# An attention and feed-forward block on one core: down weights scaled by the gate row once and kept in memory, three more copy buffers, fewer warming matmuls in the first stage

## The chip, the core and the metric

The kernel runs on one core of one Trainium2 chip. A core has a matrix engine (TensorE, PE in the profile), a vector engine (VectorE, DVE), an engine for functions such as exp (ScalarE, ACT), GpSimd (POOL) and SyncE (SP), which issues nearly all transfers here. The metric is the device time of one execution in microseconds; less is better. The time given for a kernel is the median of several executions.

## The reference, cut to what matters

One transformer block with 2048 tokens of width 512, 32 heads of 16 columns, a feed-forward width of 1792, and six modulation rows that come from a condition `c`. All inputs are bfloat16.

```python
mod = (_silu(c) @ w_mod).reshape(1, 6, 1, -1)
sa, ca, ga, sb, cb, gb = (mod[:, k] for k in range(6))
h = _layernorm(x) * (1 + ca) + sa
q, k, v = heads(h @ wqkv)                       # 32 heads of 16 columns
p = softmax(q @ k.T / 4)
x = x + ga * ((p @ v) @ wo)
h = _layernorm(x) * (1 + cb) + sb
x = x + gb * ((gelu(h @ w_gate) * (h @ w_up)) @ w_down)
```

The change touches the last line. `gb` is a row of 512 numbers that multiplies the columns of the product with `w_down`, so it can be multiplied into the columns of `w_down` just as well.

## The kernel before

**Stages.** The prologue (`prologue`, from line 524) loads x, the modulation weights and the first columns of `wqkv`, normalises four token tiles, computes `sa` and `ca` as columns (`mod_cols`), transposes, and projects the first queries and keys. Matmuls on a zero tile (`warm_up`: 5, 11, 4 and 3 of them, 512 columns each) stand between its parts. Then `stream` runs through 2048 score tiles (128 keys by 512 columns) in a fixed order: first the pairs of heads of the first 512 queries, then query sets of 256 tokens, at last two sets of 128 (`SETS`, nine sets, numbered 0 to 8). A "round" is four such tiles, one for each of four heads that share the array. `tail` finishes the last set.

**Two ways to the exponential.** Most score tiles are taken out of PSUM by ScalarE, two or three tiles to an ACTIVATE (`E<-ps_sc`, line 341). Some rounds are given to VectorE instead. Such a round, called a vector round below (`quad` in the code), is four TENSOR_SCALARs of 128x512, which turn each score into the bits of a bfloat16 power of two (into a buffer of `self.kq`), and three TENSOR_SCALARs of 128x2048, which make three shifted copies of those bits (`shift_task`, each into a buffer of `self.sq`, the copy buffers). The product with v is then done four times, on the bits and on the three copies with three scaled versions of v (`vs`), which averages out the error of the cheap exponential. A copy buffer comes free when its product has been issued.

**The copy buffers.** There are six: three in `mreg`, one of its own, one in `ereg` and one in the upper half of `onorm`. `room` in `stream` says which may be used: numbers 3, 4, 5 for the first two units, 3 and 4 until the second modulation is computed, and then 0 to 3, with number 4 for the first four units as well.

**The order of the work** is decided when the program is built. A planner in `stream` keeps a modelled clock for each engine (`model`, `cost`) and takes at each step the work that could run then: the next score tiles, a product with v, or one step of the side work (`plan`: projections, the output projection `side_wo`, the feed-forward `side_ffn`), which has a credit that grows with the tiles done. Steps for VectorE and for the transfers wait in a list of tasks (`task`), sorted by `urgency`. A new vector round is begun only if VectorE is free soon, its list is short, a `kq` buffer is free, and no other condition in that long `elif` forbids it. The instructions then run in that order on each engine, with semaphores.

**The feed-forward.** Sets 0 to 5 (`FLOW` is 6) run while the attention of later sets still needs the memory, so for each of them the gate, up and down weights are loaded again from HBM in pieces (`load`, `load_down`; a down piece is 256 rows, 256 KB, into `wdst`). Sets 6 to 8 use weights that stay in memory, loaded late by `weight_parts`. The gate row is applied in two ways. For sets 0 to 5 `down_fin` multiplies the 128x512 result in PSUM by `gb` into `xw` and adds `xw` to x. For sets 6 to 8 `scale_down` multiplies the fourteen resident 128x512 tiles of down weights by `gb` on VectorE when they have arrived (tasks `("wds", i)`), and `down_fin` adds the PSUM result to x directly.

```python
    def down_fin(self, bank, t, flow=False):
        if flow:
            self.tt("dve", self.xw, bank, self.gb[:, :], ALU.mult)
        self.tt("dve", self.xs[:, t, :], self.xs[:, t, :], self.xw if flow else bank, ALU.add)
```

The seventh pieces of the resident gate and down weights go to `hreg`, behind the products of the feed-forward, and may be loaded after set 0's feed-forward (in the run: around 612 and 620 us); pieces 4 to 6 of the up weights and piece 5 of the down weights wait for set 5's feed-forward (around 701 us).

Of the kernel before, what the change touches and what calls it, by code (L numbers as in the profile page):

```python
# [6 lines left out]
ALU = mybir.AluOpType  # L7
BF16 = mybir.dt.bfloat16
# [40 lines left out]
AHEAD = (30, 44)  # L49
FLOW = sum(a + n <= 1536 for a, n in SETS)  # L50
URGENT = 9
LATE = 2
# [8 lines left out]
TUNE = ((600, 3500, 6, 120),) * 16  # L61
# [31 lines left out]
class _Recorder:  # L93
# [167 lines left out]
    def model(self, op, t, cost):  # L261
# [6 lines left out]
        elif eng == "pe":  # L268
# [11 lines left out]
            end = t + max(cols + (12 if mode else 6), 64) / 2.4  # L280
# [153 lines left out]
class _Kernel(_Recorder):  # L434
# [12 lines left out]
    def alloc(self):  # L447
# [40 lines left out]
        self.sq += [ereg[:, :], onorm[:, 2048:4096]]  # L488
# [6 lines left out]
        self.xw = self.gw[:, 0, 0, 0:D]  # L495
# [19 lines left out]
        self.ones = dreg[:, 10 * D:10 * D + P]  # L515
        self.half = dreg[:, 10 * D + P:10 * D + 2 * P]
# [4 lines left out]
        self.scr2 = self.dram("scr_rec", [4, 2048], FP32)  # L521


    def prologue(self):
# [52 lines left out]
        self.warm_up(4)  # L577
        self.mod_cols(self.scp[:, 1, 0:8], 0, range(4))
        self.warm_up(3)
# [347 lines left out]
    def weight_parts(self):  # L927
# [5 lines left out]
        dv = self.B_w_down.rearrange("(f p) n -> p f n", p=P)  # L933
# [7 lines left out]
        return ([piece(0, i, g[i]) for i in range(6)] + [piece(0, 6, g[6], [("ffn", 0)]), piece(2, 6, d[6], [("ffn", 0)])]  # L941
# [20 lines left out]
    def scale_down(self):  # L962

        for i in range(NFC // 2):
            self.task([lambda fc=fc: self.tt("dve", self.wd[fc // 2][:, fc % 2, :], self.wd[fc // 2][:, fc % 2, :], self.gb[:, :], ALU.mult)
                       for fc in (2 * i, 2 * i + 1)], ("wds", i), self.after([("wr", 2, i)]))

# [144 lines left out]
    def side_ffn(self, gi, part=None):  # L1112
# [116 lines left out]
        for i in range(n):  # L1229
            for fc in range(NFC):  # L1230
                yield from self.until(("wl", gi, 2, fc // 2) if flow else ("wds", fc // 2))
                yield 512, lambda i=i, fc=fc: self.mm(
                    mi, prod[:, fc, P * i:P * i + P], (self.wdst if flow else self.wd)[fc // 2][:, fc % 2, :], start=(fc == 0), stop=(fc == NFC - 1))
            self.down_fin(mi, tiles[i], flow)
# [8 lines left out]
    def urgency(self, tk):  # L1243
# [3 lines left out]
        if tk[1] is not None and tk[1][0] == "shift" and self.plain[tk[1][1]] <= LATE:  # L1247
            return -2
# [774 lines left out]
```

## Time and profile before

| | |
|---|---|
| median of 3 runs | 818.45 us (818.15 to 819.36) |
| span of the profiled execution, first to last instruction | 817.5 us |
| ACT busy | 783.2 us (96%) |
| PE busy | 750.5 us (92%) |
| DVE busy | 742.8 us (91%) |
| mean granted TensorE clock | 1.000 |
| DMA, mean over the span | 70 GB/s |

The profile gives the profiled execution by its span alone, which is 0.95 us below the median of the runs. In the rows, a line is "start, length, engine, source line, operation, output<-input, shape, count", and a bracket tells how long the engine was idle before it and what ended that. Tiles are called by the memory they lie in: `E<-ps_sc` is ScalarE's exponential; `dreg`, `kq`, `mreg` or `onorm` `<-ps_sc` with 128x512 uint16 is the first part of a vector round; 128x2048 uint16 is one of its three copies; `wreg<-ps_mi,gb` is the multiplication in `down_fin`, and `xs<-xs,gb` and `hreg<-hreg,gb` are those of `scale_down`. Nearly every operation goes through a helper, so the source line names the helper (328 is a matmul, 341 an ACTIVATE, 353 a TENSOR_SCALAR, 345 a TENSOR_TENSOR), and groups are told apart by their tiles.

### The profile page before, as it was taken

What the parts mean: (1) busy time and instruction counts of PE and PEld (TensorE: products, weight loads), DVE (VectorE), ACT (ScalarE), POOL (GpSimd) and SP (SyncE); (2) the same over time, 40 slices, a digit from 0 to 9 for tenths busy, and PEclk for the clock granted to TensorE, in tenths of its full rate; (3) what the DMA queues carried; (4) which work ended last, traced back from release to release, by engine and by line L of the source; (5) the groups of instructions that cost most, each with busy time, mean ns of one, the idle gap of its engine ahead of it and who ended that gap; (6) DMA issues with size and microseconds to landing.
All of it is one profiled execution on the core that took longest, in us unless ns stands there. A gap on an engine that the chain in (4) does not pass through costs nothing.

```text
span 817.5 us, 37365 instructions
## 1 busy us (share of the span) xinstructions
PE 750.5 (92%) x17184; PEld 366.4 (45%) x17188; DVE 742.8 (91%) x1496; ACT 783.2 (96%) x746; POOL 4.6 (1%) x13
## 2 busy tenths in 40 slices
PE   7899999998999898989999899998998899888998
PEld 3333334343543454435443444444443444346567
DVE  6876898899999999999999999999999999989874
ACT  5999999999999999999999999999999999999962
POOL 2000000000000000000000000000000000000000
PEclk9999999999999999999999999999999999999999
DMA  9100000021530153104420442034233541200000
GB/s 292 63 6 20 10 9 10 10 71 40 168 112 16 52 155 93 35 21 134 122 63 16 136 121 61 16 105 133 63 106 88 165 126 36 67 10 10 19 13 14
DMA packets 94499, 57.38 MB, mean 70 GB/s; under 512 B 17029, under 2 KB 91910, under 8 KB 94342
## 3 DMA queue, kind: packets, MB, share of 16 engines
q1 hardware_dynamic: 93812, 54.47, 23.6%
q8 instruction: 134, 2.20, 1.2%
q10 hardware_dynamic: 530, 0.53, 0.2%
q14 instruction: 23, 0.19, 0.1%
HBM read 50.04 MB, written 2.35 MB: 64 GB/s over the span
## 4 chain that ended last, share of the span: by engine, by line
ACT 88%; PE 9%; DVE 1%; issue 0%; DMA 0%; SPq 0%; DVEq 0%
ACT E L341 85%; PE ps_sc L328 4%; PE ps_mi L328 3%; ACT wreg L341 3%; PE ps_pv L328 2%; DMA xs<-in_A_x_dram 0%; DVE osb L362 0%; DVE xs L345 0%; DVE dreg L353 0%; DVE st L381 0%; DVE wreg L353 0%; DVE nwt L345 0%; PE ps_sc L332 0%; DVE wreg L358 0%; DVE mreg L353 0%
## 5 line engine op out<-in xcount | busy, mean ns | idle before, releaser
L341 ACT ACTIVATE E<-ps_sc 128x1024 bf16<-128x1024 f32 (+2 forms) x700 | 758.7, 1319 | 19.1 <-PE ps_sc L328 19.0
L328 PE MATMUL ps_sc<-qT,kT 32*128 32x256 bf16 (+3 forms) x2048 | 202.2, 273 | 25.2 <-ACT E L341 21.1
L328 PE MATMUL ps_sc<-qo,kT 32*128 32x256 bf16 (+2 forms) x2048 | 202.2, 273 | 16.9 <-ACT E L341 15.5
L328 PE MATMUL ps_pv<-E,vaug 128*17 128x256 bf16 (+2 forms) x3204 | 154.1, 273 | 3.8 <-DVE osb L362 2.7
L353 DVE TENSOR_SCALAR dreg<-ps_sc 128x512 uint16<-128x512 f32 x200 | 135.5, 687 | 6.8 <-PE ps_sc L328 5.8
L328 PE MATMUL ps_mi<-wreg,mreg 128*32 128x256 bf16 x2816 | 116.6, 275 | 6.5 <-DVE wreg L362 3.4
L328 PEld LDWEIGHTS ps_sc<-qT,kT 32*128 32x128 bf16 (+1 forms) x2048 | 62.3, 92 | 117.3 <-ACT E L341 105.1
L328 PEld LDWEIGHTS ps_sc<-qo,kT 32*128 32x128 bf16 x2048 | 62.1, 92 | 105.6 <-ACT E L341 94.9
L328 PEld LDWEIGHTS ps_pv<-E,vaug 128*17 128x17 bf16 x3204 | 60.4, 89 | 59.6 <-issue 39.8
L328 PEld LDWEIGHTS ps_mi<-wreg,mreg 128*32 128x32 bf16 x2816 | 63.7, 96 | 42.8 <-issue 24.8
L328 PE MATMUL ps_pv<-mreg,vs 128*17 128x256 bf16 (+2 forms) x1840 | 80.9, 268 | 0.6 <-DVE mreg L353 0.3
L353 DVE TENSOR_SCALAR kq<-ps_sc 128x512 uint16<-128x512 f32 x104 | 70.9, 688 | 8.6 <-PE ps_sc L328 8.2
L353 DVE TENSOR_SCALAR mreg<-dreg 128x2048 uint16<-128x2048 uint16 x100 | 67.5, 682 | 2.2 <-PE ps_pv L328 2.2
L353 DVE TENSOR_SCALAR mreg<-ps_sc 128x512 uint16<-128x512 f32 x96 | 65.0, 688 | 4.5 <-PE ps_sc L328 4.3
L328 PEld LDWEIGHTS ps_pv<-mreg,vs 128*17 128x17 bf16 x1840 | 40.7, 91 | 15.1 <-issue 4.7
L353 DVE TENSOR_SCALAR mreg<-mreg 128x2048 uint16<-128x2048 uint16 x71 | 47.4, 686 | 0.0
L328 PE MATMUL ps_mi<-hreg,wreg 128*32 128x512 bf16 (+1 forms) x496 | 36.6, 376 | 0.4 <-DVE vaug L362 0.3
L362 DVE CAST wreg<-ps_mi 128x512 bf16<-128x512 f32 x49 | 33.6, 686 | 2.4 <-PE ps_mi L328 2.2
L345 DVE TENSOR_TENSOR wreg<-wreg 128x1024 bf16<-128x1024 bf16 (+1 forms) x56 | 34.5, 618 | 0.0
L353 DVE TENSOR_SCALAR sq<-dreg 128x2048 uint16<-128x2048 uint16 x49 | 33.7, 687 | 0.8 <-PE ps_pv L328 0.8
L358 DVE SCALAR_TENSOR_TENSOR wreg<-wreg,ps_mi 128x512 bf16<-128x512 bf16 x49 | 33.4, 682 | 1.0 <-ACT wreg L341 0.5
L353 DVE TENSOR_SCALAR mreg<-kq 128x2048 uint16<-128x2048 uint16 x48 | 32.5, 683 | 0.0
(193 smaller groups left out, 722.7 us busy)
## 6 DMA issues: line engine op xcount, KB each, us to landing
mreg<-in_B_w_up_dram SPq DMA_DIRECT2D x46, 256.0 KB, 3.2
mreg<-in_B_w_gate_dram SPq DMA_DIRECT2D x42, 256.0 KB, 3.3
dreg<-in_B_w_down_dram SPq DMA_DIRECT2D x18, 256.0 KB, 3.5
rb<-scr_rec SPq DMA_DIRECT2D x120, 32.0 KB, 2.0
mreg<-in_B_w_down_dram SPq DMA_DIRECT2D x12, 256.0 KB, 3.7
ereg<-in_B_w_down_dram SPq DMA_DIRECT2D x12, 256.0 KB, 3.8
mreg<-in_w_mod_dram SPq DMA_DIRECT2D x1, 2048.0 KB, 11.8
out_dram<-xs SPq DMA_DIRECT2D x15, 128.0 KB, 1.7
```

The lines of the kernel that those rows point to most:

```text
L328: return self.rec("pe", lambda e: e.matmul(out, lhsT, rhs, start=start, stop=stop, tile_position=tp), [lhsT, rhs], [out], cost=(n, int(rhs ...
L341: return self.rec("act", lambda e: e.activation(out, in_, func, scale=scale, **kw), rd, wr, cost=self.cost("act", out, [in_], "act"))
L345: return self.rec(eng, lambda e: e.tensor_tensor(out, a, b, op), [a, b], [out], cost=self.cost(eng, out, [a, b], "tt"))
L353: return self.rec(eng, lambda e: e.tensor_scalar(out, a, s1, s2, **kw), rd, [out], cost=self.cost(eng, out, [a], "ts") + 60 * (len(rd) - 1 ...
L358: return self.rec("dve", lambda e: e.scalar_tensor_tensor(out, a, s, b, op0=op0, op1=op1), rd, [out], cost=self.cost("dve", out, [a, b], " ...
L362: return self.rec(eng, lambda e: e.tensor_copy(out, in_), [in_], [out], cost=self.cost(eng, out, [in_], "ts"))
```

## The change

- **Down weights.** Set 0's feed-forward loads the down weights as before, multiplies each of the seven pieces in place by `gb` (two TENSOR_TENSORs of 128x512 a piece), and stores the piece to a new tensor `wd_scaled` in HBM. Sets 1 to 5 and the resident copy load from there. `scale_down` is gone, and `down_fin` adds PSUM to x directly for every set.
- **Copy buffers.** Three more: number 6 in `hreg` behind the products, 7 in the part of `mreg` that is down buffers 3 and 4, and 8 in the part of `dreg` that is down buffers 1 and 2. Rules say when each may be used: 8 is added to the early lists and, with 4, to the list until the last query projection is done; 6 is added from there to the end of set 5's feed-forward; 4 and 7 after that. Set 0's loads of down pieces 1, 2, 5 and 6 wait until numbers 8 and 4 are free. The seventh resident gate and down pieces now wait for the end of set 5's feed-forward and for number 6. The constants `ones` and `half` move out of `dreg` to tiles of their own.
- **First stage.** Of the last three warming calls (11, 4 and 3 matmuls) 11 and 1 are left.
- **The planner.** The model takes a full-array matmul as at least 158 columns long (it was 64 for all kinds). The planner's constants are gathered in a tuple that may differ for every 64 score tiles; all its entries have the values of before.

```diff
-        self.sq += [ereg[:, :], onorm[:, 2048:4096]]
+        self.sq += [ereg[:, :], onorm[:, 2048:4096], hreg[:, NFC * 256:NFC * 256 + 2048], mreg[:, 10240:12288], dreg[:, 10 * D:14 * D]]
...
-            end = t + max(cols + (12 if mode else 6), 64) / 2.4
+            end = t + max(cols + (12 if mode else 6), 64 if mode else 158) / 2.4
...
         self.warm_up(11)
         self.mod_cols(self.scp[:, 1, 0:8], 0, range(4, 8))
-        self.warm_up(4)
+        self.warm_up(1)
         self.mod_cols(self.scp[:, 1, 0:8], 0, range(4))
-        self.warm_up(3)
         self.ln_rstd(0, 4)
...
-        return ([piece(0, i, g[i]) for i in range(6)] + [piece(0, 6, g[6], [("ffn", 0)]), piece(2, 6, d[6], [("ffn", 0)])]
+        return ([piece(0, i, g[i]) for i in range(6)] + [piece(0, 6, g[6], [last, "sq"]), piece(2, 6, d[6], [last, "sq"])]
...
-    def down_fin(self, bank, t, flow=False):
-        if flow:
-            self.tt("dve", self.xw, bank, self.gb[:, :], ALU.mult)
-        self.tt("dve", self.xs[:, t, :], self.xs[:, t, :], self.xw if flow else bank, ALU.add)
+    def down_fin(self, bank, t):
+        self.tt("dve", self.xs[:, t, :], self.xs[:, t, :], bank, ALU.add)
...
-                v = self.B_w_down.rearrange("(f p) n -> p f n", p=P)
-                self.task([("sp", lambda: self.dma("sp", self.wdst[i], v[:, 2 * i:2 * i + 2, :], "sd%d" % i))], ("wl", gi, 2, i))
+                v = self.wdg if gi else self.B_w_down.rearrange("(f p) n -> p f n", p=P)
+                steps = [("sp", lambda: self.dma("sp", self.wdst[i], v[:, 2 * i:2 * i + 2, :], "sd%d" % i))]
+                if not gi:
+                    steps += [lambda x=x: self.tt("dve", self.wdst[i][:, x, :], self.wdst[i][:, x, :], self.gb[:, :], ALU.mult) for x in range(2)]
+                    steps += [("sp", lambda: self.dma("sp", self.wdg[:, 2 * i:2 * i + 2, :], self.wdst[i], "ws%d" % i))]
+                self.task(steps, ("wl", gi, 2, i),
+                          (lambda: NSQ in self.sq_free) if i > 4 else (lambda: NSQ + 4 in self.sq_free) if i in (1, 2) else None)
...
             if u in units[:2]:
-                ok = (3, 4) if pool is self.quad_free else (3, 4, 5)
+                ok = (3, 4) if pool is self.quad_free else (3, 4, 5, 8)
             elif "modB" not in self.have:
-                ok = (3,) if pool is self.quad_free else (3, 4)
+                ok = (3,) if pool is self.quad_free else (3, 4, 8)
+            elif pool is self.quad_free:
+                ok = range(NK)
             else:
-                ok = range(NK if pool is self.quad_free else NSQ + (u in units[:4]))
+                ok = list(range(NSQ))
+                if ("ffn", FLOW - 1) in self.have:
+                    ok += [NSQ, NSQ + 3]
+                elif ("q", 3, NDC - 1) in self.have:
+                    ok += [NSQ + 2]
+                elif ("t2T", 0) not in self.have:
+                    ok += [NSQ, NSQ + 4]
```

More of the change, by code (lines that the diff above doesn't have):

```diff
@@ L514, in alloc @@
         self.zero = sb("zero", [P, P], BF16)
-        self.ones = dreg[:, 10 * D:10 * D + P]
-        self.half = dreg[:, 10 * D + P:10 * D + 2 * P]
+        self.ones = sb("ones", [P, P], BF16)[:, :]
+        self.half = sb("half", [P, 2], BF16)[:, :]
         self.self32 = sb("self32", [P, P], FP32)
@@ L960, in scale_wo @@
         yield
[L962 to L966, printed above, removed]
     def normed(self, k, i):
@@ L1246, in urgency @@
             return -3
-        if tk[1] is not None and tk[1][0] == "shift" and self.plain[tk[1][1]] <= LATE:
+        if tk[1] is not None and tk[1][0] == "shift" and self.plain[tk[1][1]] <= self.tune[6]:
             return -2
@@ L1293, in background @@
             pass
-        while self.free["dve"] <= t + 150 and self.step("dve", max(self.free["dve"], t) + 40):
+        while self.free["dve"] <= t + self.tune[13] and self.step("dve", max(self.free["dve"], t) + 40):
             pass
@@ L1547, in stream @@
         parts = self.weight_parts()
-        self.scale_down()
         while cg <= group[units[-1]]:
+            if ("ffn", FLOW - 1) in self.have and NSQ + 2 in self.sq_free:
+                self.done("sq")
             if parts and pos >= max(loaded, ends[FLOW - 1] + 8):
@@ L1557, in stream @@
             t = max(self.pe_now(), virt)
-            self.tune = TUNE[min(pos // P, 15)]
+            if pos // STEP != stage:
+                stage = pos // STEP
+                self.rules(stage)
             for k in range(NSETS):
```

40 lines of the change are left out of this document (21 added, 19 removed).

## The prediction

> **What bounds the kernel now.** I read the page's head and its chain first, then the chain in order of time, then a table by stage, since the shares of the whole run (ACT 96%, PE 92%, DVE 91%) leave open which engine sets the time where.
>
> ```profile
> span 817.5 us, 37365 instructions
> ACT 88%; PE 9%; DVE 1%; issue 0%; DMA 0%; SPq 0%; DVEq 0%
> ...
> 16.45 101.58 ACT E L341 x93
> ...
> 669.72 60.76 ACT E L341 x56
> ...
> 736.01 5.45 ACT E L341 x5
> 741.50 0.62 PE ps_sc L328 x12
> ```
>
> ```profile
> core 0: us, PE busy (x) PEld busy (x) DVE busy (x) ACT busy (x) POOL busy (x), PEclk, DMA share, GB/s
> 40.00:100.00 60.00, 55.50 (x1036) 20.90 (x1036) 44.98 (x102) 60.00 (x57) 0.31 (x1) 1.00 0.05 12
> 100.00:200.00 100.00, 93.96 (x2115) 39.94 (x2114) 91.85 (x174) 99.02 (x92) 0.00 (x0) 1.00 0.10 23
> 200.00:700.00 500.00, 464.17 (x10794) 223.77 (x10791) 484.19 (x913) 500.00 (x476) 0.00 (x0) 1.00 0.32 89
> 700.00:740.00 40.00, 34.59 (x832) 17.83 (x832) 35.19 (x73) 40.00 (x36) 0.00 (x0) 1.00 0.14 40
> 740.00:790.00 50.00, 45.45 (x1620) 29.37 (x1612) 42.11 (x91) 46.37 (x43) 0.00 (x0) 1.00 0.07 13
> ```
>
> There are three stages. Up to 16.45 us a chain of all engines leads to the first exponentials. From there to 741 us ScalarE is busy without a pause, but for 1 us near 118, so the time of this stage is the sum of ScalarE's work. From 741.5 the chain runs through TensorE, and ScalarE has gaps (46.37 busy of 50). In the long middle stage only less work for ScalarE shortens the run, and such work can only go to VectorE, by vector rounds. Whether more of them are made depends on VectorE: it is full from 200 to 700 (484.19 of 500) but idle for 15.0 us between 40 and 100 and for 8.2 us between 100 and 200.
>
> **The price of a vector round.**
>
> ```profile
> L341 ACT ACTIVATE E<-ps_sc 128x1024 bf16<-128x1024 f32 x432 | 434.9, 1169 | 2.0 <-PE ps_sc L328 2.0
> L341 ACT ACTIVATE E<-ps_sc 128x1536 bf16<-128x1536 f32 x260 | 385.9, 1591 | 3.8 <-PE ps_sc L328 3.8
> ```
>
> ```profile
> L328 PE MATMUL ps_pv<-mreg,vs 128*17 128x256 bf16 (+2 forms) x1840 | 80.9, 268 | 0.6 <-DVE mreg L353 0.3
> L353 DVE TENSOR_SCALAR kq<-ps_sc 128x512 uint16<-128x512 f32 x104 | 70.9, 688 | 8.6 <-PE ps_sc L328 8.2
> L353 DVE TENSOR_SCALAR mreg<-dreg 128x2048 uint16<-128x2048 uint16 x100 | 67.5, 682 | 2.2 <-PE ps_pv L328 2.2
> ```
>
> In a step with a vector tile the ACTIVATE has two tiles in place of three: 1591 - 1169 = 422 ns less. A round is four tiles, so it takes 4 x 0.422 = 1.69 us from ScalarE. It costs VectorE 4 x 0.688 + 3 x 0.682 = 4.80 us. It costs TensorE three more products with v; at width 256 these are 24 matmuls of 80.9/1840 = 0.044 us, 1.06 us.
>
> **The change part by part.**
>
> *Warming matmuls (six of seven gone).*
>
> ```profile
> 8.67 1.02 PE L328 MATMUL ps_mi<-dreg 128*128 128x512 bf16 x4
> 9.53 0.54 PE L328 MATMUL ps_sc<-sc_bf,mreg 128*128 128x1 bf16 x16
> 10.15 0.59 PE L328 MATMUL ps_mi<-dreg 128*128 128x512 bf16 x2
> 10.58 0.72 PE L332 MATMUL ps_sc<-ident,dreg 128*128 128x128 bf16 x10
> ```
>
> ```profile
> DMA to landing us min/median/max: 6.8/6.9/7.0
> ```
>
> ```profile
> 1.81 0.47 SPq L391 DMA_DIRECT2D mreg<-in_w_mod_dram  x1
> ...
> 8.52 1.05 DVE L353 TENSOR_SCALAR dreg<-xs,mv,rstd 128x512 bf16<-128x512 bf16 x3
> ...
> 8.63 0.81 ACT L341 ACTIVATE dreg<-xs,nwt,rstd 128x512 bf16<-128x512 bf16 x1 [2.98 <-DVE nwt L358]
> ...
> 11.85 0.28 PE L328 MATMUL ps_sc<-hreg,wreg 128*128 128x256 bf16 x1 [0.21 <-ACT hreg L341]
> ...
> 14.33 1.45 ACT L341 ACTIVATE E<-ps_sc 128x1536 bf16<-128x1536 f32 x1 [0.58 <-PE ps_sc L328]
> ```
>
> These matmuls lie on the chain. The second half of the modulation columns (9.53) waits for four of them, the transposes (10.58) for the other three. Without them that half waits for its weights: issued at 1.81 us and landing 7.0 us later (the row on landing gives the two such transfers), at 8.8 us, so it starts near 8.9 and ends near 9.45. The transposes then wait for the normalised tiles, ready at 9.57 on VectorE and 9.44 on ScalarE. They start near 9.55 and not 10.58: 1.0 us less to the first exponential, now at 14.33. The ends are 0 (something later, such as the query weights, binds) and 1.03; I take 1.0, since the row nearest to a limit, the tiles at 9.57, has been counted.
>
> The trace shows the clock rise during the 11 matmuls that stay: their lengths fall from 634 to 380 ns.
>
> ```profile
> L328 PE MATMUL ps_mi<-dreg x6: 608/634/634, 3.7 to 5.8; 128*128 128x512 bf16 x6
> ...
> L328 PE MATMUL ps_mi<-dreg x3: 379/380/427, 7.1 to 7.6; 128*128 128x512 bf16 x3
> ```
>
> The Trainium skill (TensorE: Matmul & The Clock Gate, Part 1) says that the clock halves again only after an idle window of about 3.4 us; by that the gain stays 1.0. Its Part 4 speaks against the change: transposes do not count as busy in the same way, and transposes take the place of the warming matmuls. Rival 3 is what that would cost here.
>
> *Multiplication by the gate row.*
>
> ```profile
> L345 DVE TENSOR_TENSOR wreg<-ps_mi,gb x12: 680/683/692, 252.9 to 699.4; 128x512 bf16<-128x512 f32 x12
> L345 DVE TENSOR_TENSOR xs<-xs,gb x12: 366/420/422, 625.3 to 713.3; 128x512 bf16<-128x512 bf16 x12
> ```
>
> The rows give the shortest, median and longest length in ns, and the first and last start. Twelve multiplications out of PSUM go: 12 x 0.683 = 8.2 us of VectorE, two per set of sets 0 to 5. The fourteen on the weights (twelve in this row, two more on the piece in `hreg`) are not removed but moved, from 625 to 713 us to set 0's feed-forward, ahead of its first result at 252.9: 14 x 0.420 = 5.9 us there, and as much less later. In both places VectorE is full, so 1.2 rounds (5.9/4.80) are lost and won, which I cost at nothing. The 8.2 us are worth 8.2/4.80 = 1.7 rounds, 2.9 us at most and 0 at least (if the planner leaves them idle). Rounds are whole and the time comes in pieces of 1.4 us per set, so I take one, 1.7 us.
>
> *Traffic for the scaled weights.*
>
> ```profile
> dreg<-in_B_w_down_dram SPq DMA_DIRECT2D x18, 256.0 KB, 3.5
> ```
>
> Seven stores of 256 KB are added on SP's queue, in a stage where the DMA share is 0.32; behind them stand the loads of the next pieces and the small transfers of the softmax sums. A load of such a piece takes 3.5 us to land, and set 1 reads the stored pieces most of a set later; a set takes about (699.4 - 252.9)/5 = 89 us. Cost nothing; without that cover one landing, 3.5 us. Set 0's down matmuls now wait for load and scaling; what hides this is the gate and up work ahead of them. The added waits for buffers 4 and 8 come after these have ceased to be given out, so they cost nothing, or again one landing.
>
> *Late pieces of the resident weights.*
>
> ```profile
> 700.95 1.98 SPq L391 DMA_DIRECT2D dreg<-in_B_w_up_dram  x1
> ...
> 720.78 0.69 DVE L362 CAST wreg<-ps_mi 128x512 bf16<-128x512 f32 x1 [1.35 <-PE ps_mi L328]
> ```
>
> Two more pieces now go ahead of the up pieces issued at 700.95, spaced by eight score tiles each, about 6 us by 2048 tiles in some 775 us. The up pieces would land near 711; set 6's feed-forward takes its first gate result at 720.78 and uses those pieces later. Nothing.
>
> *Copy buffers.* Three or four in place of two or three before 95 us, six in place of four or five up to about 185 us, five in place of four until 700, then six. Where VectorE is full they add nothing. Between 40 and 200 us it is idle for 23.2 us, room for 4 whole rounds (23.2/4.80), 6.8 us; at least 0, and less than nothing is excluded by TensorE's idle time there (4.5 + 6.0 us against 1.06 a round). How much of the idle time is due to buffers can't be read directly:
>
> ```profile
> 87.46 0.69 DVE L353 TENSOR_SCALAR ereg<-kq 128x2048 uint16<-128x2048 uint16 x1
> ...
> 88.95 0.69 DVE L353 TENSOR_SCALAR sq<-kq 128x2048 uint16<-128x2048 uint16 x1
> ```
>
> Here the third copy of a round came 0.8 us late, into the buffer that the first had left, so the buffers do bind, if shortly; most of the gaps wait for TensorE. By that nearest row I take one round, 1.7 us.
>
> *The planner's 158 columns* move no work, only its order; I take 0, with an end of one ACTIVATE, 1.6 us, to either side.
>
> **The sum.** 1.0 + 1.7 + 1.7 = 4.4 us less: a span of 813.1, and with the 0.95 us by which the span lies below the median of the runs, 814.0.
>
> **The rivals.**
>
> 1. *The end grows.* From 741 us TensorE sets the time, and a vector round there gives nothing to it and costs. With six buffers in place of four, more rounds find room: VectorE has 4.8 us idle from 700 to 740 and 7.9 from 740 to 790, enough for two whole rounds.
>
> ```profile
> L328 PE MATMUL ps_pv<-mreg,vs 128*17 128x128 bf16 (+1 forms) x216 | 5.4, 221 | 0.0
> ...
> DVE mreg L353 <- PE ps_pv L328: 2.1, 1, 2.1
> ```
>
> At width 128 a round costs TensorE 48 x 5.4/216 = 1.2 us, and at most all its 4.80 us on VectorE, if they stand ahead of the feed-forward's steps for which TensorE waits. Two rounds are 2.4 to 9.6 us; the forecast is eaten up and the run is slower by 0.2% from 3.0 us a round. Taking 4.0, the time is 822. For it: copies waited for a buffer here (2.1 us). Against: at 1.2 us it does not decide.
>
> 2. *Nothing is made of it.* VectorE's freed time and the buffers bring no round, because the begin of a round is forbidden by other conditions. Then only the first stage gains: 817.5. For it: most idle time of VectorE before 100 us ends with TensorE, not with a buffer.
>
> 3. *The clock falls back* after the transposes. From the transposes at 10.58 to the first exponential at 14.33 are 3.75 us; were all of them TensorE's, they would take 634/380 as long, 2.5 us more: 816.5. Against it: the matmul of 256 columns at 11.85, right after the transposes, takes 0.28 us, which is not a slow length beside 0.38 for 512.
>
> 4. *Much more of it.* All four rounds before 200 us and two from the freed time: 818.45 - 1.0 - 6 x 1.69 = 807.3.
>
> **How the numbers follow.** The forecast has 0.48, rival 1 0.24, rival 2 0.14, rival 3 0.04, rival 4 0.10. Within 0.2% (1.6 us) is about what a measurement of this kernel can't tell from no change; so faster is 0.48 + 0.04 + 0.10 = 0.62, same 0.14, slower 0.24. The forecast's own range is 811 to 816.5 (one round more or none, 1.6 us of order). For 8 in 10 it reaches to rival 1 at 822 and towards rival 4, to 808.5, which leaves out about half of each beyond.
>
> **What would show it.** The first exponential should start near 13.3 and not 14.33. The rows with `ps_mi,gb` should be gone, and fourteen of 0.42 us stand before 253 us. The TENSOR_SCALARs of 128x512 uint16 out of `ps_sc` should be 8 more than before (two rounds), and the ACTIVATEs of 1536 columns fewer. ScalarE's unbroken stretch should end 4 us earlier, near 737, and the last 76 us keep their length. The prediction is wrong if the count of rounds falls, or if that last stretch grows by 4 us or more.

## The result, and the profile after

The changed kernel is slower by 0.3%: 822.23 us, the median of 20 runs (819.64 to 827.39), against 819.42 us for the kernel before beside it (20 runs, 818.15 to 823.71); the ratio is 1.0032, with a 95% interval of 1.0017 to 1.0047. Forecast were 814.0 us, and the time lies just above the end of the range, 822.0. The profiled execution is one of the best of the changed kernel: 819.71 us, a span of 818.0 us at a mean granted clock of 0.998, against a span of 817.5 at 1.000 before.

The page's head, its busy times and the shares of its chain:

```profile
span 818.0 us, 37375 instructions
...
PE 749.4 (92%) x17194; PEld 366.7 (45%) x17194; DVE 737.7 (90%) x1484; ACT 783.6 (96%) x746; POOL 4.6 (1%) x13
...
ACT 76%; PE 17%; DVE 5%; DMA 1%; issue 1%; SPq 0%; DVEq 0%
```

The chain names ScalarE for 76% of the span; before it was 88%. Yet ScalarE has the same work as before (783.6 us against 783.2), and VectorE has 5.1 us less (737.7 against 742.8). The groups by shape show what became of the freed time: every kind of exponential has its old count.

```profile
L340 ACT ACTIVATE E<-ps_sc 128x1024 bf16<-128x1024 f32 x432 | 434.7, 1169 | 7.3 <-PE ps_sc L327 7.2
L340 ACT ACTIVATE E<-ps_sc 128x1536 bf16<-128x1536 f32 x260 | 384.4, 1597 | 2.3 <-PE ps_sc L327 2.3
...
L352 DVE TENSOR_SCALAR dreg<-ps_sc 128x512 uint16<-128x512 f32 x200 | 134.7, 684 | 10.4 <-PE ps_sc L327 9.6
L352 DVE TENSOR_SCALAR kq<-ps_sc 128x512 uint16<-128x512 f32 x104 | 70.2, 684 | 8.7 <-PE ps_sc L327 8.2
L352 DVE TENSOR_SCALAR mreg<-ps_sc 128x512 uint16<-128x512 f32 x96 | 64.6, 683 | 3.0 <-PE ps_sc L327 2.4
...
L352 DVE TENSOR_SCALAR onorm<-ps_sc 128x512 uint16<-128x512 f32 x4 | 2.7, 672 | 1.6 <-PE ps_sc L327 1.6
```

200 + 104 + 96 + 4 are 404 tiles, 101 rounds, as many as before. No round has been made of VectorE's freed time or of the new buffers. What changed on ScalarE is the wait: 7.3 us ahead of the ACTIVATEs of 1024 columns, where it was 2.0 (ahead of those of 1536 columns 2.3, where it was 3.8). The table by stage (same columns as before) shows where:

```profile
40.00:100.00 60.00, 54.59 (x1016) 20.33 (x1008) 44.77 (x103) 60.00 (x57) 0.31 (x1) 1.00 0.05 12
100.00:200.00 100.00, 94.24 (x2151) 40.80 (x2152) 92.89 (x177) 98.12 (x91) 0.00 (x0) 1.00 0.10 23
200.00:700.00 500.00, 461.25 (x10764) 223.49 (x10760) 478.09 (x897) 497.59 (x473) 0.00 (x0) 1.00 0.33 91
700.00:740.00 40.00, 36.34 (x868) 18.11 (x867) 36.00 (x75) 40.00 (x37) 0.00 (x0) 1.00 0.20 53
740.00:790.00 50.00, 45.77 (x1574) 29.18 (x1568) 42.18 (x92) 46.66 (x43) 0.00 (x0) 1.00 0.07 16
```

Between 40 and 740 us ScalarE, unbroken before but for 1 us, is now idle for 1.88 + 2.41 = 4.29 us. The start and the end of the exponentials, from the timeline (start, length):

```profile
7.84 0.54 PE L327 MATMUL ps_sc<-sc_bf,mreg 128*128 128x1 bf16 x16
...
8.65 1.03 PE L331 MATMUL ps_sc<-ident,dreg 128*128 128x128 bf16 x10 [0.27 <-DVE dreg L352]
...
12.71 1.45 ACT L340 ACTIVATE E<-ps_sc 128x1536 bf16<-128x1536 f32 x1 [0.58 <-PE ps_sc L327]
...
792.08 1.28 ACT L340 ACT_TABLE_LOAD   x1
```

The kernel before has the same table load, behind its last exponential, at 789.52:

```profile
789.52 1.28 ACT L341 ACT_TABLE_LOAD   x1
```

So the profiled executions compare like this. The first exponential is 1.62 us earlier (12.71 against 14.33). ScalarE loses 4.29 - 0.98 = 3.3 us more to waits between 40 and 740, and 0.7 us in a stretch of halved clock near 21 us (below). Its own work is 0.4 us longer and its idle time from 740 to 790 is 0.3 shorter. That makes 2.5 us, and the end of the exponentials is 2.56 us later. From there to the end the changed kernel needs 25.9 us and not 28.0, which leaves the 0.5 us between the spans.

Most of the middle stage's loss lies in one stretch. Counted by the starts of the instructions that take score tiles out of PSUM, the changed kernel is 0.2 us ahead at tile 512 and 3.3 us behind at tile 704. Of the 192 tiles between, VectorE takes 38 and not 43, which is 5 x 0.42 = 2.1 us more for ScalarE, and ScalarE waits for 1.25 us, where it did not wait before. From tile 1536 to 1920 VectorE takes 84 tiles and not 78, so that the count of the whole run is the same.

### The profile page after: what moved, and what is told of

Its sections match the earlier page's. It is cut to its first block, busy times and chain, and to the rows that moved or that the text cites. A ratio compares the mean times of both kernels' runs of the same rounds, so it can differ in the third digit from the quotient of the medians.

```text
span 818.0 us, 37375 instructions
## 1 busy us (share of the span) xinstructions
PE 749.4 (92%) x17194; PEld 366.7 (45%) x17194; DVE 737.7 (90%) x1484; ACT 783.6 (96%) x746; POOL 4.6 (1%) x13
## 4 chain that ended last, share of the span: by engine, by line
ACT 76%; PE 17%; DVE 5%; DMA 1%; issue 1%; SPq 0%; DVEq 0%
ACT E L340 73%; PE ps_sc L327 7%; PE ps_mi L327 6%; PE ps_pv L327 4%; ACT wreg L340 3%; DVE dreg L352 1%; DVE mreg L352 1%; DVE kq L352 1%; DMA scr_rec<-rden 1%; DMA xs<-in_A_x_dram 0%; DVE wreg L361 0%; DMA rb<-scr_rec 0%; DVE wreg L357 0%; DVE st L380 0%; DVE osb L361 0%
## 5 line engine op out<-in xcount | busy, mean ns | idle before, releaser
L327 PE MATMUL ps_sc<-qT,kT 32*128 32x256 bf16 (+3 forms) x2048 | 193.7, 273 | 26.3 <-ACT E L340 22.2
L327 PE MATMUL ps_sc<-qo,kT 32*128 32x256 bf16 (+2 forms) x2048 | 193.4, 273 | 15.0 <-ACT E L340 13.6
L327 PEld LDWEIGHTS ps_sc<-qT,kT 32*128 32x128 bf16 (+1 forms) x2048 | 59.6, 92 | 117.8 <-ACT E L340 103.3
L327 PEld LDWEIGHTS ps_sc<-qo,kT 32*128 32x128 bf16 x2048 | 59.5, 92 | 103.9 <-ACT E L340 90.6
L327 PE MATMUL ps_pv<-mreg,vs 128*17 128x256 bf16 (+2 forms) x1472 | 62.8, 268 | 1.0 <-DVE mreg L352 0.9
L352 DVE TENSOR_SCALAR mreg<-dreg 128x2048 uint16<-128x2048 uint16 x90 | 60.3, 680 | 0.0
L327 PEld LDWEIGHTS ps_pv<-mreg,vs 128*17 128x17 bf16 x1472 | 32.9, 91 | 11.1 <-issue 4.0
L352 DVE TENSOR_SCALAR mreg<-mreg 128x2048 uint16<-128x2048 uint16 x47 | 31.7, 682 | 0.0
L361 DVE COPY osb<-ps_pv 128x256 f32<-128x256 f32 (+2 forms) x63 | 25.9, 412 | 5.5 <-PE ps_pv L327 5.4
L340 ACT ACTIVATE wreg<-wreg 128x1024 bf16<-128x1024 bf16 (+1 forms) x28 | 30.8, 1099 | 0.0
```

What stands on the lines that cost most here:

```text
L327: return self.rec("pe", lambda e: e.matmul(out, lhsT, rhs, start=start, stop=stop, tile_position=tp), [lhsT, rhs], [out], cost=(n, int(rhs ...
L340: return self.rec("act", lambda e: e.activation(out, in_, func, scale=scale, **kw), rd, wr, cost=self.cost("act", out, [in_], "act"))
L352: return self.rec(eng, lambda e: e.tensor_scalar(out, a, s1, s2, **kw), rd, [out], cost=self.cost(eng, out, [a], "ts") + 60 * (len(rd) - 1 ...
L361: return self.rec(eng, lambda e: e.tensor_copy(out, in_), [in_], [out], cost=self.cost(eng, out, [in_], "ts"))
```

## The experiments

Each kernel ran several times beside the kernel before on the same chip; a ratio is to that, with its 95% interval, and below 1 is faster. "Planned again" says that the planner ran again and was free to make a new order of the whole kernel; "order kept" says that instructions were taken out or put in after the planning and all others stayed in place.

### Each part of the change by itself

The modelled columns, undone in the changed kernel (e1), and alone in the kernel before (e2):

```diff
-            end = t + max(cols + (12 if mode else 6), 64 if mode else 158) / 2.4
+            end = t + max(cols + (12 if mode else 6), 64 if mode else 64) / 2.4
```

> The changed kernel with one thing undone: the planner's model takes a full-array matmul as at least 64 columns again, as before. The work is the same, only its order is planned anew. Theory R (the new order, brought about by the 158 columns, costs the time): about 3 us less than the changed kernel, near 819 us. Theory C (the missing warming matmuls let TensorE's clock fall) and theory S (the scaling in set 0's stage costs the time): as the changed kernel, near 822 us, with a mean granted clock near 0.994.

> The kernel before with one thing of the change alone: 158 columns in the planner's model. Theory R: 3 to 5 us slower than before, near 823 us, with fewer vector rounds than 101. Theories C and S: within 1 us of before, 819.4.

e1 took 821.40 us, 1.0015 (0.9995 to 1.0034), with 102 rounds, which can be told neither from the kernel before nor from the changed one. e2 took 825.86 us, 1.0068 (1.0046 to 1.0089), with 99 rounds. This constant belongs to the planner's model and to no instruction, so it only orders the work; but the order also decides how many rounds VectorE gets, and e2's two fewer rounds leave ScalarE more to do (788.0 us against 783.2). Alone the constant costs more than the whole change does.

Fewer warming matmuls alone (e3), planned again, and the changed kernel with them back (e4):

```diff
-        self.warm_up(4)
+        self.warm_up(1)
...
-        self.warm_up(3)
```

> The kernel before with one thing of the change alone: six of the last seven warming matmuls left out. Theory C: the first exponential starts 1.6 us earlier (12.7 in place of 14.3 us), but the mean granted clock falls below 0.997 in most executions and the time is 1 to 3 us above before, near 821. Theories R and S: the 1.6 us are kept, 817.8 us, with the clock as in the kernel before.

> The changed kernel with one thing undone: the calls of 4 and 3 warming matmuls are back. Theory C: the first exponential is 1.6 us later, at 14.3 us, but the clock stays above 0.997 in most executions; the median is near 821, below that of the changed kernel (822.2), and the executions lie closer together. Theories R and S: the 1.6 us are added and nothing is won back, 823.8 us.

e3 took 820.93 us, 1.0022 (1.0000 to 1.0044), at a mean granted clock of 0.9931, which is what theory C expected, but in a new order. e4 took 823.10 us, 1.0032 (1.0014 to 1.0051). In e4 the planner happened to arrive at the order of the changed kernel: VectorE, ScalarE and the transfers have the same instructions in the same order, and so has TensorE but for ten more matmuls in the first stage, six of warming and four that fill. So e4 tests the matmuls of the first stage alone, and its clock, 0.9945, is as low as the changed kernel's 0.9942. The missing warming matmuls do not cause the lower clock.

The scaled down weights alone (e5) and the three copy buffers alone (e6), both on the kernel before and planned again:

```diff
-                v = self.B_w_down.rearrange("(f p) n -> p f n", p=P)
+                v = self.wdg if gi else self.B_w_down.rearrange("(f p) n -> p f n", p=P)
...
+                if not gi:
+                    steps += [lambda x=x: self.tt("dve", self.wdst[i][:, x, :], self.wdst[i][:, x, :], self.gb[:, :], ALU.mult) for x in range(2)]
+                    steps += [("sp", lambda: self.dma("sp", self.wdg[:, 2 * i:2 * i + 2, :], self.wdst[i], "ws%d" % i))]
```

```diff
-        self.sq += [ereg[:, :], onorm[:, 2048:4096]]
+        self.sq += [ereg[:, :], onorm[:, 2048:4096], hreg[:, NFC * 256:NFC * 256 + 2048], mreg[:, 10240:12288], dreg[:, 10 * D:14 * D]]
```

> The kernel before with one part of the change alone: the down weights scaled once in set 0's feed-forward, stored and read back. Theory S (the fourteen multiplications land on a full VectorE in set 0's stage): between score tile 512 and 768 the run falls 2 to 4 us behind the kernel before, fewer than 101 vector rounds, near 822 us. If S is wrong the 8 us less of VectorE's work show: 818 to 820 us (before 820.2).

> The kernel before with one part of the change alone: the three copy buffers with their rules. If buffers held back vector rounds, there are 102 or more and the time is 817 to 819 us. If not (rival 2 of the prediction), 100 to 101 rounds, and any difference is one of order (theory R), up to 3 us to the slow side by the clock: 820 to 823 us.

e5 took 819.90 us, 1.0011 (0.9992 to 1.0029), with 98 rounds. e6 took 822.72 us, 1.0040 (1.0026 to 1.0054), with 100. Neither makes a round more than before. The parts' losses, 0.7, 0.2, 0.1 and 0.4%, do not add up to the 0.3% of the whole either, so they aren't prices of the parts: each edit also gave another order.

### How much is the order alone?

One nanosecond in the latency that the planner assumes for ScalarE, in the kernel before (e8) and in the changed one (e9):

```diff
-                    op.t1 = t + cost + (107 if eng == "act" else 92)
+                    op.t1 = t + cost + (108 if eng == "act" else 92)
```

> The kernel before with a change that has no meaning for the work: the planner takes ScalarE's results to be ready 108 and not 107 ns after an operation. Theory R with W (any new order loses what this one order has): mean clock 0.993 to 0.996 in place of 0.997, and 821 to 823 us. If the parts of the change are to blame by themselves: 820 us and a clock of 0.997, as the kernel before.

> The changed kernel with the meaningless change that was made to the kernel before (ScalarE's results taken to be ready after 108 and not 107 ns). Theory R (order alone moves the time by some us either way): any value from 819 to 825 us. If the parts of the change set the time: 822.2 us as the changed kernel, within 0.8.

e8 took 818.86 us, 0.9991 (0.9979 to 1.0003), and e9 819.77 us, 1.0011 (0.9993 to 1.0029). For e9 this is 2.4 us less than the changed kernel by the medians, but the intervals of the two overlap. The instructions of e9 are those of the changed kernel, in the same order, up to about 540 us; its mean clock is 0.9973 against 0.9942, and straight lines of the span over the clock (see below) put both at 817 us at full clock. So this pair says little of order as such; what differs in it is the clock.

Then both kernels got the same other constants for the planner (e11 the changed one, e12 the one before). They were chosen among 150 settings because with them the planner's model ended earliest for the changed kernel, and e11's model takes 64 columns again, as that of the kernel before does:

```diff
-FILL = 3700
+FILL = 3800
-RULES = (600, 3500, 6, 120, 700, 150, 2, 9, 96, 30, 2, 1536, 100, 150)
+RULES = (600, 3500, 6, 120, 800, 100, 2, 10, 128, 30, 1, 1536, 95, 150)
```

> The changed kernel with the planner's limits set anew (seven constants, and 64 columns in the model), chosen among 150 settings because the planner itself puts this order's end earliest. No work is added or removed but filler matmuls. Theory R: 816 to 818 us, below the kernel before, with a clock of 0.996 or more and 101 vector rounds. If the parts of the change are slower by themselves: 820 us or more.

> The kernel before with the same constants as the one just named, so that the two differ by the parts of the change alone. Theory R: this setting was found for the other kernel, so here it is an order like any other: 820 to 823 us. If the setting is good by itself, whatever the kernel: 816 to 818 us, as the other.

e11: 1.0005 (0.9987 to 1.0023). e12: 1.0070 (1.0052 to 1.0088). With these constants the changed kernel, but for its 158 columns, is the faster one by 0.65%, though e11 is no faster than the kernel before with its own constants (821.43 us, where 816 to 818 were expected). The settings were picked for one of the two, so this is no fair price of the change; but it shows that the sign of the comparison hangs on the order that each of the two gets.

### What forbids a round, and what a round is worth

When the changed kernel is built, one can count at how many of the places where a round could begin a condition was the only one against it. A list of VectorE's tasks that is too long (six or more) was the commonest: 14 of 38 places at tiles 512 to 768, 22 of 73 at 1024 to 1536. Before tile 256 the scaled versions of v were missing at 26 of 37 places, though mostly together with something else (alone at 4). A free copy buffer isn't among the conditions. e10 raises the limit of the list in the changed kernel:

```diff
-RULES = (600, 3500, 6, 120, 700, 150, 2, 9, 96, 30, 2, 1536, 100, 150)
+RULES = (600, 3500, 14, 120, 700, 150, 2, 9, 96, 30, 2, 1536, 100, 150)
```

> The changed kernel with one limit raised: a vector round may begin when VectorE's list of pending steps is shorter than 14, in place of 6. Theory L (this limit, not copy buffers or VectorE's time, held the number of rounds at 101): 103 or more rounds. If a round more is worth the 1.69 us of the prediction, the time falls by 3 to 5 us, to 817 to 819. If the rounds come at the cost of the feed-forward's steps on VectorE (theory F), the number rises and the time does not fall: 822 us or more.

It made 104 rounds, three more, and took 832.19 us, 1.0148 (1.0116 to 1.0180). Its profiled execution ran at full clock. The page's head, the table by stage and the table load:

```profile
span 824.2 us, 37402 instructions
...
PE 752.1 (91%) x17198; PEld 369.5 (45%) x17202; DVE 747.7 (91%) x1505; ACT 778.4 (94%) x746; POOL 4.6 (1%) x13
```

```profile
100.00:200.00 100.00, 93.68 (x2102) 40.37 (x2103) 91.69 (x174) 96.98 (x90) 0.00 (x0) 1.00 0.09 23
200.00:700.00 500.00, 461.96 (x10756) 224.01 (x10760) 483.90 (x912) 493.83 (x473) 0.00 (x0) 1.00 0.33 91
```

```profile
789.48 1.28 ACT L340 ACT_TABLE_LOAD   x1
```

ScalarE has 783.6 - 778.4 = 5.2 us less to do, 1.73 us for each of the three rounds: that part of the price was right. But it waits for 3.02 + 6.17 = 9.2 us between 100 and 700 (the changed kernel 4.3, the one before 1.0), so the exponentials end at 789.48, no sooner than in the kernel before. Then 34.7 us follow, where it was 28.0. The costliest matmuls of the last stretch, from 790 us on, show what was left for it, first in e10, then in the kernel before:

```profile
L327 PE MATMUL ps_mi<-xs,hreg 128*128 128x512 bf16 x33 | 7.9, 379 | 1.2 <-DVE xs L344 0.8 <-DVE osb L361 0.4
```

```profile
L328 PE MATMUL ps_mi<-xs,hreg 128*128 128x512 bf16 x10 | 2.3, 379 | 0.1
```

33 matmuls of a feed-forward in place of 10 came after the last exponentials. VectorE also serves the feed-forward, and what it does for a round it does not do for that; that the rounds pushed these matmuls back is the likely reading, though no run shows it by itself.

### The clock

Every timed execution comes with its span and its mean granted clock. Over the 20 executions of the changed kernel the mean clock is 0.9942, over 138 of the kernel before, taken beside e1 to e18, 0.9972. A straight line through the spans of each kernel gives 642 and 485 us per unit of clock, and at full clock 817.0 and 816.4 us. What a fall is can be seen in the profiled execution of the changed kernel, in stretches around its only one:

```profile
16.29:19.70 3.41, 2.30 (x34) 0.60 (x22) 2.91 (x12) 3.41 (x4) 0.00 (x0) 1.00 1.05 393
19.70:23.11 3.41, 3.41 (x28) 1.21 (x25) 2.78 (x10) 3.04 (x3) 0.00 (x0) 0.50 1.02 384
```

and in the kernel before at the same place:

```profile
16.29:19.70 3.41, 2.93 (x86) 1.40 (x84) 2.64 (x10) 3.25 (x4) 0.00 (x0) 1.00 1.07 386
```

For 3.41 us the clock is 0.50, after 3.41 us in which TensorE had been busy for 2.30 us (before: 2.93, and no fall). One fall of this length takes 0.5 x 3.41/820 = 0.0021 off the mean clock, 1.0 to 1.3 us by the slopes. Counted in falls of this length, the kernel before has 1.3 in an execution (0.0028/0.0021) and the changed one 2.8 (0.0058/0.0021). ScalarE felt this one in two waits, of 0.36 and 0.34 us:

```profile
22.08 1.02 ACT L340 ACTIVATE E<-ps_sc 128x1024 bf16<-128x1024 f32 x1 [0.36 <-PE ps_sc L327]
23.45 1.45 ACT L340 ACTIVATE E<-ps_sc 128x1536 bf16<-128x1536 f32 x1 [0.34 <-PE ps_sc L327]
```

The busy time is not what decides. In e3's profile the clock falls after a stretch in which TensorE was busy for 3.00 us:

```profile
83.92:87.33 3.41, 3.00 (x60) 1.47 (x56) 2.45 (x7) 3.41 (x4) 0.00 (x0) 1.00 0.36 61
87.33:90.74 3.41, 3.41 (x30) 0.68 (x27) 2.38 (x4) 2.51 (x3) 0.00 (x0) 0.50 0.00 0
```

The columns that TensorE works through say more, if a matmul on a quarter of the array is counted as a quarter. In every profile the rises and falls lie whole multiples of 3.41 us apart. On that grid, between 7 and 790 us of all twenty profiles, 14 stretches at full clock have fewer than 2800 columns, and each is followed by a fall. Of 88 with 2800 to 3328 columns 16 are, and of the more than 4000 above none is. (Matmuls of 512 columns at full clock, one every 0.216 us, would make some 8100 columns in such a stretch.) So it is thin work, and not idle time as such, that goes with the falls. Where the grid lies differs from profile to profile. Averaged over all places that it could have, the profile of the changed kernel has 2.6 stretches of fewer than 3000 columns and that of the kernel before 1.4, close to the 2.8 and 1.3 falls above: the changed kernel's order has more of them.

If thin stretches are the cause, filling them must bring the clock back. e7 lets the planner put more filling matmuls in, planned again:

```diff
-FILL = 3700
+FILL = 4100
```

> The changed kernel with the planner's limit for filler matmuls raised from 3700 to 4100 columns in 3.41 us, so that TensorE is kept busier in weak places. Theory W (the granted clock halves for 3.41 us where TensorE was given fewer than some 3100 columns in a window of that length, and the changed order has more such places): mean clock 0.996 or more in place of 0.994, and a time of 820.5 to 822, not slower than the changed kernel (822.2). If the falls of the clock have another cause: clock 0.994 as there, and 823 to 824 us by the fillers' own cost.

e7 took 822.52 us, 1.0039 (1.0026 to 1.0052), at a clock of 0.9977, with 99 rounds: the clock was better, the time was not. So in e13 and e14 the order was kept, and groups of four matmuls with zero weights were put in wherever TensorE had less than 4000 columns of work in 3.41 us: 144 groups in the changed kernel, 152 in the one before.

```diff
+                        return e.matmul(acc[32 * j:32 * j + VW, 0:W], self.zero[:, 0:VW], rhs, start=False, stop=False, tile_position=(0, 32 * j))
```

> The changed kernel with its order of instructions as it is, and 144 groups of four matmuls on zero weights put in after the planning, ahead of products with v in places where the planned TensorE work is under 4000 columns in 3.41 us. They add nothing to the sums. Theory W: the mean clock rises from 0.994 to 0.997 or more and the time falls from 822.2 to about 820.3, since each fall of the clock costs about 1.3 us; the executions lie closer together. If the clock isn't a cause: 822 to 824 us.

> The control: the kernel before with the same treatment (152 groups). Theory W: its clock is at 0.997 already, so there is little to win: 819 to 820.5 us beside 819.7, clock 0.998. If zero matmuls help or hurt for another reason, it shows here: more than 1 us either way.

| | median, us | ratio (interval) | mean clock | standard deviation, us | at full clock, us |
|---|---|---|---|---|---|
| changed | 822.23 | 1.0032 (1.0017 to 1.0047) | 0.9942 | 2.3 | 817.0 |
| changed, filled (e13) | 821.36 | 1.0022 (1.0010 to 1.0034) | 0.9982 | 0.9 | 819.3 |
| before (138 executions) | 819.78 | | 0.9972 | 1.3 | 816.4 |
| before, filled (e14) | 822.54 | 1.0037 (1.0023 to 1.0052) | 0.9987 | 1.5 | 821.1 |

("At full clock" is the span from the straight line.) With the order kept, more work for TensorE brings the clock from 0.9942 to 0.9982 and the scatter from 2.3 to 0.9 us. The changed kernel gets no slower by it, while the kernel before loses 2.8 us to the same kind of matmuls. This fits a low clock that costs time, but does not show it by itself, since by the lines the matmuls also cost the two kernels unlike amounts at full clock, 2.3 and 4.7 us. That a fall costs time is seen in the two waits above and in the slopes within one kernel. As a cure the filling is no good: e13 took 821.4 us where 820.3 were expected.

The same filling was tried on the two best orders so far, that of e11 (e15, 123 groups) and that of e8 (e16, 143 groups):

> The changed kernel with the limits set anew (821.4 us at a clock of 0.9946; its executions at a full clock have a span of 816.0), with the same treatment (123 groups). Theory W: clock 0.997, 818 us or less, below the kernel before. Otherwise 821 us or more.

> The kernel before planned with 108 ns (818.9 us, clock 0.9959), with the same treatment (143 groups). Theory W: clock 0.998 and 817 to 818 us. Otherwise 819 us or more.

e15: 1.0016 (1.0000 to 1.0032) against 1.0005 for e11; e16: 1.0000 (0.9985 to 1.0015) against 0.9991 for e8. The clock rose both times (to 0.9977 and 0.9987), and neither got faster, where 818 us or less were expected.

### The first stage with the order kept

What the six warming matmuls are worth can be measured without a new plan. They are taken out after the planning, from the kernel before (e17) and from e8 (e18):

```diff
+        self.ops = [op for op in self.ops if op not in self.spare_mm]
...
-        for _ in range(n):
-            self.mm(self.mi[:, :], self.warm[:, 0:P], self.warm)
+        ops = [self.mm(self.mi[:, :], self.warm[:, 0:P], self.warm) for _ in range(n)]
+        self.spare_mm = {5: [], 11: [], 4: ops[1:], 3: ops}[n] + getattr(self, "spare_mm", [])
```

> The kernel before with the six warming matmuls taken out after the planning, so that every other instruction keeps its place. The prediction's term for this edit (1.0 us, the changed kernel's first exponential is 1.6 us earlier): 818.1 us if the gain is kept to the end, with a clock of 0.997 as in the kernel before. If the missing matmuls let the clock fall in the first stage: 819 to 821 us and a clock of 0.995 or less.

> The kernel before as planned with 108 ns (818.9 us), with the same six matmuls taken out after the planning. If the gain is kept: 817.2 us, below the kernel before. Otherwise 819 us or more, with a clock under 0.995.

The first exponential of e17:

```profile
13.02 1.45 ACT L341 ACTIVATE E<-ps_sc 128x1536 bf16<-128x1536 f32 x1 [0.58 <-PE ps_sc L328]
```

It starts 1.31 us earlier than in the kernel before. Part of that is the transfer of the modulation weights, which landed 6.8 to 7.0 us after its issue in the profile of the kernel before (the row is in the prediction), and in that of e17 sooner:

```profile
DMA to landing us min/median/max: 4.9/5.5/6.1
```

Nine profiles are of kernels with all warming matmuls: in eight the first exponential starts at 13.30 to 14.33 us, and in e14's, where the clock falls at 11.14, at 16.56. In the eleven without the six it starts at 12.71 to 13.32. Without e14's the medians, 13.75 and 13.06, are 0.7 us apart.

e17 took 818.41 us, 0.9990 (0.9976 to 1.0004), and e18 817.15 us, 0.9973 (0.9958 to 0.9988), against 818.86 us for e8. By the medians the edit is worth 1.6 us (e17 against the kernel beside it, 819.98) and 1.7 (from e8 to e18); but e17's ratio is 0.8 us, with an interval that still holds no change, and the profiles give 0.7. So the gain is about 1 us, known to within 1 us. e18 is faster than both kernels of the change.

## Why the prediction was wrong

The forecast, 814.0 us, is 8.2 us off. 1.0 of that is the kernel before, 819.42 us in the runs beside the changed kernel and 818.45 in the three that the sum started from. 4.4 are the forecast gain, which does not show in the time, and 2.8 the loss. Two steps failed: the two rounds (3.4 us) were never made, and the new order, put at 0 with ends of 1.6 us, was a larger term than that: it brought ScalarE 3.3 us of waits, and a lower clock of TensorE, 1.5 to 1.9 us by the straight lines.

**The warming matmuls (a gain of 1.0 us): right.** The profiles give 0.7 us at the first exponential, the times about 1 us. In the profile of the changed kernel the transposes start at 8.65, not 9.55, and the first exponential at 12.71. The half of the modulation columns that the sum let wait for its weights until 8.9 ran at 7.84: the bound came from one profile, and the same transfers land 4.7 to 5.8 us after their issue in this one.

**The gate row: moved as described, but worth less.**

```profile
L344 DVE TENSOR_TENSOR dreg<-dreg,gb x6: 415/416/419, 212.2 to 216.3; 128x512 bf16<-128x512 bf16 x6
L344 DVE TENSOR_TENSOR mreg<-mreg,gb x4: 415/415/416, 217.2 to 229.8; 128x512 bf16<-128x512 bf16 x4
L344 DVE TENSOR_TENSOR ereg<-ereg,gb x4: 410/414/418, 231.6 to 242.0; 128x512 bf16<-128x512 bf16 x4
```

The rows of the tile `gb` have fourteen multiplications of 0.415 us between 212.2 and 242.0 and none out of PSUM. But VectorE has 5.1 us less to do, not the 8.2 of the sum, which left something out. The additions to x took the product from SBUF and now take it out of PSUM, which is slower. First the kernel before, then the changed one:

```profile
L345 DVE TENSOR_TENSOR xs<-xs,wreg 128x512 bf16<-128x512 bf16 x12 | 5.1, 425 | 0.4
```

```profile
L344 DVE TENSOR_TENSOR xs<-xs,ps_mi 128x512 bf16<-128x512 bf16 x30 | 20.4, 679 | 5.6 <-PE ps_mi L327 5.6
```

Twelve of the thirty are these: 12 x (0.679 - 0.425) = 3.0 us, so that the freed time was worth 1.1 rounds and not 1.7.

**Vector rounds from freed time and from the buffers (1.7 us each): wrong.** There are 404 such tiles, as before. Room on the engine isn't all that the planner asks for. It also looks at the length of its list, at the scaled versions of v in the early stretch that the forecast counted on, and at no copy buffer. Raising the limit of the list alone brought three rounds (e10), the buffers alone none (e6). Rival 2 named this, with 0.14. The row used for the buffers (a third copy 0.8 us late) was a delay inside a round, no obstacle to the next one.

**The price of a round (1.69 us of ScalarE's time): true for the work, wrong for the time.** e10 made three more rounds and was slower by 12 us, 6.7 of them in the spans of two executions at full clock. The sum took it that a shorter sum of ScalarE's work shortens the middle stage. It did not: the saved 5.2 us came back as waits of ScalarE for score tiles, and the last stretch grew by 6.7 us, with feed-forward left over. That growth is the mechanism of rival 1, at its place and by the feed-forward that its upper price named, but in e10 alone: in the changed kernel no round was added and the last stretch got 2.1 us shorter. That rival 1's 822 us are nearly the measured time is luck.

**The new order (cost 0, ends of 1.6 us): the largest miss.** The prediction gave that term to the 158 columns alone. But each edit of instructions or costs has the planner order the whole kernel anew. Constants of the planner alone took the time from no clear change to 0.7% above the kernel before (e8, e2, e12), up to about 6 us. ScalarE's 3.3 us of new waits in the changed kernel are, it seems, of this kind: the clock is 1.00 in those stretches, its work is the same, and TensorE and VectorE have no more to do than before. The fourteen multiplications in set 0's stage are no good explanation: from tile 512 to tile 704 the kernel before needed 70.0 us and the changed one 73.5, but e2, e3 and e6, which don't have them there, needed 72.9 to 74.0, and e5, which does, 71.1.

**The clock (rival 3, 0.04): the right engine, mostly at another place.** In the changed kernel's profile the clock fell at 19.70, 10 us behind the transposes; other falls come later, where the matmuls are sparse. A fall right at the transposes does occur, but in e14's profile, where all warming matmuls are in place (the clock is 0.50 from 11.14 to 14.55). The changed kernel's mean clock is lower by 0.0030, 1.5 to 1.9 us by the two slopes; e4, which has the same order, shows the same low clock. Of the 2.8 us between the medians 0.6 us is left at full clock by the lines, or 1.2 us between the medians of the executions with a clock of 0.997 and more (818.2 and 817.0). The share rests on the lines.

The Trainium skill (TensorE: Matmul & The Clock Gate, Part 1), on which the prediction relied for a gain that stays, says that the clock halves after an idle window of about 3.4 us. The length agrees with the grid of 3.41 us on which the falls start here. The condition does not: TensorE was busy for 2.30 of the 3.41 us before the fall.

What stays open: which part of the change gave its order the 3.3 us of waits, or whether any did, and which part gave it more thin stretches. With the settings of e11 and e12, picked for it, the change is 0.65% faster, with its own it is 0.3% slower, and two pairs are too few for a price of the change without its order.

## What to carry to other kernels

Where a planner writes the order, an edit that makes it plan again is measured together with a new order, and constants of the planner alone moved the time here by up to 6 us; take the edit out or put it in with the order kept (as e17 did), or compare several orders of both kernels. Freed time of an engine is worth nothing until the rule that gives out its work binds on that engine, so read the rule's conditions and raise the one that binds before counting on it. And give the mean clock beside each time: by the lines more than half of the loss here was the clock.

## What was unexpected of the hardware

The granted clock falls to exactly one half, mostly for 3.41 us, and TensorE need not be idle for it: the stretch before was 67% busy (2.30 of 3.41 us) in the changed kernel, and 88% (3.00) in e3. What the falls follow is a stretch with fewer than some 3000 columns of matmul work, where about 8100 would fit. Some last longer: in e18's profile the clock stays at 0.50 from 14.69 to 28.34 us. It also falls late in the run; e4's profile has one near 682 us:

```profile
681.94:685.35 3.41, 3.27 (x32) 0.70 (x32) 2.35 (x6) 2.60 (x4) 0.00 (x0) 0.50 0.64 170
```

The same kernel differs from run to run: the profiled execution of the kernel before had no fall at all, though its mean over 138 executions is 1.3. And zero-weight matmuls, which change no result and keep the clock up, are not free: 144 to 152 groups of four cost 2.3 to 4.7 us at full clock, by the lines, in a kernel whose TensorE is 92% busy.
